# An outer-product recurrence and a bilinear feed-forward in one kernel: weights put together as integers, first units' f loaded whole, and a reordered beginning

## The chip, the cores and the metric

The kernel runs on one core of one Trainium2 chip. A core has a matrix engine (PE, TensorE), a vector engine (DVE), an activation engine (ACT), a general engine (POOL) and a queue engine (SP) that issues most of the transfers. SBUF is the on-chip memory of 128 partitions, PSUM the memory that PE writes to. The metric is device microseconds for one execution, from the first to the last instruction with what lies around it; lower is better.

## The reference

For each of 4 batches and 8 heads a state of 48 by 48 runs through 768 time steps; the outputs of all heads, side by side, are the rows of a feed-forward that multiplies two projections.

```python
f = 1.0 / (1.0 + np.exp(-f_logit))
for t in range(S):
    state = f[:, :, t, :, None] * state + np.einsum('bhd,bhe->bhde', k[:, :, t], v[:, :, t])
    y[:, :, t] = np.einsum('bhd,bhde->bhe', q[:, :, t], state)
x = y.transpose(0, 2, 1, 3).reshape(B * S, H * D)      # 3072 x 384
out = ((x @ w_a) * (x @ w_b)) @ w_out                  # w_a, w_b: 384 x 1536, w_out: 1536 x 384
```

The three weights arrive as 64-bit floats (the random fp32 times a double factor), all else as fp32.

## The kernel before

**The recurrence without a loop over time.** Within a half sequence of 384 steps (BLK), the running product F of f turns the recurrence into plain products: q is multiplied by F, k by a quantity `inv` near 1/F, and then a causal product of q and k (`scores`, masked by `causal`), times v (`within`), plus q times the state at the start of each 64 steps (`across`) gives y. A *unit* is one batch, one half, and four heads (two pairs, the pair on partitions 0 to 47 and 64 to 111). There are 16 units, NQ = 2 of them to a half. Units 0 and 1 are the first halves of batch 0, units 2 and 3 the second halves.

Each unit goes through these steps:

- `front(u)`, a generator in three parts: ACT takes 1 - f and f as two sigmoids (L234, L235) and POOL scales `inv` (L237); DVE scans f into F, in place (L242), and compares its end (`held`, L243); DVE scans `inv` (L252) and multiplies q and k (L253, L254).
- `scores(u)` on PE (L283) and the masking on DVE (L299, tile `at`); `turn(u)`, which transposes k on PE (L310) and copies it with ACT (`kT`, L312).
- `within(u)` on PE (L363); `gains(u)`: PE computes what each 64 steps add to the state (L329), and DVE sums these one after the other into `st` (L343, L345), scaled at the end of a first half by F's last value (L352).
- `across(u)` on PE (L384); ACT copies y out of PSUM (four or three copies, L396), and transfers carry y into `xT`, the transposed input of the feed-forward (L410). For units 0 and 1 some of these are issued by ACT, all others by SP.

**The feed-forward.** A block is one half of one batch: 384 rows. `up(blk, ft)` makes the two projections for 128 of the 1536 columns: 3 + 3 matmuls in fp32, which PE runs as 12 instructions (L426), into two PSUM banks out of four that `scores`, `turn` and `within` of the first units share. `product()` copies one with ACT (`b_sb`, L441) and multiplies on DVE (L446). `down` multiplies pairs of 128 rows by w_out in Strassen-like combinations (L483, L478).

**The weights.** [...]each weight is taken from its two 32-bit words. A list `todo` of 20 pieces, (w_b, w_a) by turns and then w_out, is loaded by `load_weights` into `raw` buffers (L166). `from_double` is a generator of two parts. The first: ACT takes the magnitude of the high word scaled down (L179), its sign (L180), and from that the sign bit (L182); POOL cuts it off at a maximum (L185). The second, on DVE: shift by three and or in the sign (L188), take the exponent (L192), multiply the low word by it (L194), and add (L195). `begin(n)` runs the first part of pieces up to n, `end(n)` the second, and `end` also orders the next load.

**The order.** `tc.manual_schedule()` means that each engine runs its instructions in the order in which the program names them. The beginning, L565 to L651, is written out by hand. After it the list `rest` names all further `up` and `down` calls; its first entry is up(1, 0). Between them, `beside()` takes attention steps out of a queue by due time, and `end(6 + ...)`, `product()` and `begin(...)` keep the weights going, about one piece for each `up`. [...]SP holds an issue back until one of eight transfer semaphores is free, so that eight transfers of SP's and ACT's queues are under way at most.

Of the kernel before, what the change touches and what calls it, by code (L numbers as in the profile page):

```python
# [24 lines left out]
R = 64  # L25
# [53 lines left out]
def by_quotients(ctx, tc, q, k, f_logit, v, moe_w_a, moe_w_b, moe_w_out, out, ident, weights, bad):  # L79
# [8 lines left out]
    NTG = BLK // 128  # L88
    NU = B * NH * NQ
    NBLK = B * NH  # L90
    NSET = 3

# [23 lines left out]
    less = fixed([128, 1], "less")  # L116
    sign = fixedp.tile([128, PIECE], BF16, tag="sign", name="sign")
# [8 lines left out]
    def load_unit(u, names="fkqv"):  # L126
# [4 lines left out]
        cols = slice(half * BLK, half * BLK + BLK)  # L131
        for nm, src in (("f", f_logit), ("k", k), ("q", q)):
            if nm not in names:
                continue
            heads = src[b].rearrange("(n two) d s -> two d n s", two=2)
            for par in range(2):
                nc.sync.dma_start(out=t[nm][R * par:R * par + D], in_=heads[par][:, 2 * qd:2 * qd + 2, cols])
# [15 lines left out]

    todo, raws, going = list(pieces()), [], []
    ended = [0]

    def load_weights(n=1):
        for _ in range(n):
            if len(raws) == len(todo):
                return  # L160
            dst, src, (k, m) = todo[len(raws)]
            raw = dst
            if src.dtype != FP32:
                raw = raw_pool.tile([128, PIECE], mybir.dt.uint64, tag="raw", name="raw")[:, 0:k * m]
                raw = raw.rearrange("p (k m) -> p k m", k=k)
            nc.sync.dma_start(out=raw, in_=src)  # L166
            raws.append(raw)

    def from_double(dst, raw, k, bit):

# [8 lines left out]
        nc.scalar.activation(h, hi.bitcast(FP32), AF.Abs, scale=HI_SCALE)  # L179
        nc.scalar.activation(sgn, hi.bitcast(FP32), AF.Sign)  # L180
# [4 lines left out]
        nc.gpsimd.tensor_scalar(h, h, HI_MAX, None, ALU.min)  # L185
        yield
        hu = h.bitcast(U32)
        nc.vector.scalar_tensor_tensor(  # L188
            out=hu, in0=hu, scalar=3, in1=bit, op0=ALU.logical_shift_left, op1=ALU.bitwise_or
        )  # L190

        nc.vector.tensor_scalar(bit, hu, 0xFF800000, None, ALU.bitwise_and)  # L192
        h, lo, power = (x.rearrange("p (k n) -> p k n", k=k) for x in (h, lo, bit.bitcast(FP32)))
        nc.vector.scalar_tensor_tensor(out=dst, in0=lo, scalar=2.0**-52, in1=power, op0=ALU.mult, op1=ALU.mult)  # L194
        nc.vector.tensor_tensor(dst, h, dst, ALU.add)  # L195
        yield

    def begin(n):

        while len(going) < min(n, len(todo)):  # L200
            i = len(going)
            dst, src, shape = todo[i]
            going.append(from_double(dst, raws[i], shape[0], bits[i % len(bits)]) if src.dtype != FP32 else iter(()))
            next(going[i], None)

    def end(n):

        while ended[0] < min(n, len(todo)):
# [3 lines left out]
            if ended[0] > 2:  # L212
# [10 lines left out]
    live = {}  # L223
    xT = {}
# [4 lines left out]
    def front(u):  # L229

        t = sets[u % NSET]
        x = halves(t["f"])
        inv = sb2.tile([128, 2 * BLK], FP32, tag="inv", name="inv")
        nc.scalar.activation(inv, x, AF.Sigmoid, bias=less, scale=-1.0, accum_out=tails[:, u:u + 1])  # L234
        nc.scalar.activation(x, x, AF.Sigmoid)  # L235
# [4 lines left out]
        for n in range(2):  # L240
            c = slice(n * BLK, n * BLK + BLK)
            nc.vector.tensor_tensor_scan(x[:, c], x[:, c], none, math.exp(MIDDLE), ALU.mult, ALU.add)  # L242
        nc.vector.tensor_tensor(held[:, u], t["f"][:, :, BLK - 1], least, ALU.is_ge)  # L243
# [3 lines left out]
        nc.vector.reciprocal(start, t["f"].rearrange("p n (c m) -> p n c m", m=C)[:, :, 0:NC - 1, C - 1])  # L247
# [5 lines left out]
        nc.vector.tensor_tensor(halves(t["q"]), halves(t["q"]), x, ALU.mult)  # L253
# [63 lines left out]
    def gains(u):  # L317
# [3 lines left out]
        last = half == NH - 1  # L321
        for n in range(2):
            for c in range(NC):
                for p in range(2):
                    if last and c == NC - 1 and p == 1:
                        continue
                    for h in range(2):
                        r = slice(SUB * p, SUB * p + SUB)
                        nc.tensor.matmul(  # L329
                            ps_x[R * h:R * h + D, p, (n * NC + c) * D:(n * NC + c) * D + D],  # L330
                            lhsT=kT[r, n, c, R * h:R * h + D],
                            rhs=t["v"][r, n, c, h * D:h * D + D],
                            start=True,
                            stop=True,
                        )
        st = sb3.tile([128, NJ, 2, D], FP32, tag="st", name="st")
        before = live[u - NQ]["st"][NJ] if half else None
        live[u]["st"] = [before]
        for j in range(NJ - 1 if last else NJ):
            c, p = divmod(j, 2)  # L340
            new = ps_x[:, p, 0:2 * NC * D].rearrange("r (n c d) -> r n c d", n=2, c=NC)[:, :, c]
            if before is None:
                nc.vector.tensor_copy(st[:, j], new)  # L343
            else:
                nc.vector.tensor_tensor(st[:, j], before, new, ALU.add)  # L345
            before = st[:, j]
            live[u]["st"].append(before)
        if not last:

            for n in range(2):  # L350
                end = t["f"][:, n, BLK - 1:BLK]
# [20 lines left out]
    def across(u):  # L372
# [22 lines left out]
        for p, e, r, rows in (*whole, (1, R, 0, D), (1, 0, R, D)):  # L395
            nc.scalar.copy(y[r:r + rows, :, p], ps[p][e:e + rows, 0:BLK].rearrange("r (o m) -> r o m", m=SUB))  # L396
# [19 lines left out]
    HFT = NFT // 2  # L416
# [109 lines left out]
    def slot(u):  # L526
# [19 lines left out]
        next(nxt, None)  # L546
        yield
# [17 lines left out]
    with tc.manual_schedule():  # L565
        nc.scalar.preload_act_table_set("sigmoid_and_others")
        for x, value in ((less, -K_EXP), (zero, 0.0), (least, math.exp(MIDDLE - DECAY_MAX)), (ones, 1.0)):
            nc.gpsimd.memset(x, value)
        for n, x in (("f", 30.0), ("k", 0.0), ("q", 0.0)):
            for u in range(NSET):  # L570
                eng = nc.vector if n == "f" or n == "q" and u == 0 else nc.gpsimd
                eng.memset(sets[u][n], x)
        for ps in (ps_x, ps_y):
            nc.scalar.copy(ps[:, :, 0:BLK], zero.unsqueeze(1).broadcast_to((128, 2, BLK)))
        load_unit(0, "f")
        load_unit(1, "f")
        load_unit(0, "kqv")
        load_unit(1, "kqv")
        load_weights(2)
        load_unit(2)  # L580
        load_weights(2)


        fronts = [front(u) for u in range(2 * NQ + 1)]
        next(fronts[0])
        next(fronts[1])
        for bit in bits:
            nc.gpsimd.memset(bit, 0)
        make_identity(nc, ident)
        nc.gpsimd.memset(causal, 1.0)  # L590
        for p in range(2):
# [3 lines left out]
            )  # L595
        next(fronts[0])
        next(fronts[0])
        next(fronts[1])
        scores(0)
        turn(0, True)  # L600
        begin(2)
        next(fronts[1])
        within(0)
        gains(0)
        next(fronts[2])
        scores(1, True)
        turn(1, True)
        across(0)
        within(1, True)
        end(1)  # L610
        gains(1)
        across(1)
        for u in range(NQ):
            load_unit(u + NSET)
            load_weights()
        end(2)
        begin(3)


        next(fronts[2])  # L620
        next(fronts[2])
        scores(2)
        turn(2, True)
        next(fronts[3])
        begin(4)
        within(2)
        end(3)
        gains(2)
        up(0, 0)
        across(2)  # L630
        next(fronts[3])
        product()
        end(4)
        begin(5)
        up(0, 1)
        next(fronts[3])
        product()
# [439 lines left out]
```

## Time and profile before

| | us |
|---|---|
| median of three runs (653.26 to 655.56) | 655.42 |
| the profiled execution, its own time | 657.89 |
| its span | 656.1 |
| PE busy | 618.1 (94%) |
| weight loads of PE busy | 446.9 (68%) |
| DVE busy | 327.7 (50%) |
| ACT busy | 174.9 (27%) |
| POOL busy | 68.9 (10%) |

The profile records one execution. A row of its instruction groups gives line, engine, operation and tiles, then how many, their busy time, the mean of one in ns, and the engine's idle time just before them with what ended it. A line of the chain of work gives a start, a length and what ran. The busy times by stretch give, after the stretch and its length, PE, weight loads, DVE, ACT and POOL, each with its count of instructions, then the granted clock of PE, the share of the transfer engines and their GB/s. Matmul records overlap, so a group's mean is longer than the distance from one matmul to the next. Idle time of an engine that nobody waits for costs nothing.

### The profile page before, as it was taken

The numbers are of one execution on the slowest core, as the hardware profiler recorded it, in microseconds if no ns is written. First come the engines' busy times: TensorE is split into PE (matmuls) and PEld (weight loads), VectorE is DVE, ScalarE is ACT, GpSimd is POOL, SyncE is SP. The second block draws the span as 40 slices with busy tenths as digits, with TensorE's granted clock in tenths as the row PEclk, the third lists the DMA queues.
The fourth block names the chain that finished last, engine by engine and source line by source line (L and its number), as shares of the span: only waits on it lengthen the run. The fifth ranks groups of instructions, "written<-read, shape, count | busy, mean of one in ns | idle before, by whom it ended". The sixth has DMA issues, their size and how long they took to land.

```text
span 656.1 us, 12293 instructions
## 1 busy us (share of the span) xinstructions
PE 618.1 (94%) x5202; PEld 446.9 (68%) x5202; DVE 327.7 (50%) x610; ACT 174.9 (27%) x312; POOL 68.9 (10%) x57
## 2 busy tenths in 40 slices
PE   1667899999999999999999999999999999999996
PEld 1554555557898666966699666865689655865696
DVE  7878699995875345351443244443363121311241
ACT  3564677531321222122200312122200122011100
POOL 6232365410110000000000000000000000000000
PEclk9966999999999999999999999999999999999999
DMA  8688556100144124040210033140000000000000
GB/s 209 172 207 238 164 169 221 68 0 1 37 106 116 37 55 91 15 104 1 63 32 35 25 79 71 22 115 0 20 1 24 26 19 19 0 26 0 1 24 30
DMA packets 30209, 43.37 MB, mean 66 GB/s; under 512 B 3776, under 2 KB 24768, under 8 KB 30144
## 3 DMA queue, kind: packets, MB, share of 16 engines
q1 hardware_dynamic: 29856, 42.19, 23.7%
q8 instruction: 43, 0.70, 0.5%
q10 hardware_dynamic: 288, 0.30, 0.2%
q14 instruction: 22, 0.18, 0.1%
HBM read 33.03 MB, written 4.72 MB: 58 GB/s over the span
## 4 chain that ended last, share of the span: by engine, by line
PE 90%; DVE 5%; DMA 2%; ACT 1%; issue 1%; POOL 0%; ACTq 0%; SPq 0%; DVEq 0%
PE f L426 57%; PE f L483 24%; PE ps_x L283 2%; PE ps_y L363 2%; PE ps_y L384 2%; PE ps_x L329 1%; DMA xT<-y 1%; DVE inv L252 1%; PE ps_x L310 1%; DVE f_in L242 1%; PE f L310 1%; DVE k_in L254 1%; DMA f_in<-in_f_logit_dram 0%; DVE h L478 0%; DVE q_in L253 0%
## 5 line engine op out<-in xcount | busy, mean ns | idle before, releaser
L426 PE MATMUL f<-xT,w_a 128*128 128x384 f32 x576 | 203.6, 490 | 5.6 <-DVE start L247 4.6
L426 PE MATMUL f<-xT,w_b 128*128 128x384 f32 x576 | 205.7, 494 | 0.0
L426 PEld LDWEIGHTS f<-xT,w_a 128*128 128x128 f32 x576 | 110.1, 191 | 83.2 <-issue 6.4
L426 PEld LDWEIGHTS f<-xT,w_b 128*128 128x128 f32 x576 | 107.8, 191 | 70.4 <-issue 1.2
L446 DVE TENSOR_TENSOR ab<-f,b_sb 128x384 f32<-128x384 f32 x96 | 53.0, 554 | 180.4 <-PE f L426 130.1
L441 ACT COPY b_sb<-f 128x384 f32<-128x384 f32 x96 | 46.0, 479 | 238.9 <-PE f L426 225.8
L483 PE MATMUL f<-raw,h 128*128 128x192 f32 x432 | 73.7, 328 | 0.0
L483 PEld LDWEIGHTS f<-raw,h 128*128 128x128 f32 x432 | 70.2, 190 | 0.5
L483 PE MATMUL f<-w_out,ab 128*128 128x192 f32 x288 | 51.1, 327 | 0.9 <-DVE u L478 0.9
L237 POOL TENSOR_SCALAR inv<-inv 128x768 f32<-128x768 f32 x16 | 16.3, 1020 | 328.1 <-ACT inv L234 328.1
L185 POOL TENSOR_SCALAR h<-h 128x768 f32<-128x768 f32 (+1 forms) x20 | 44.0, 2202 | 61.3 <-ACT h L179 61.3
L483 PEld LDWEIGHTS f<-w_out,ab 128*128 128x128 f32 x288 | 47.4, 190 | 3.0 <-DVE u L478 1.2
L478 DVE TENSOR_TENSOR o<-f,u 128x192 f32<-128x192 f32 x36 | 12.9, 357 | 56.6 <-PE f L483 56.4
L283 PE MATMUL ps_x<-q_in,k_in 48*64 48x64 f32 x720 | 16.2, 238 | 22.1 <-DVE k_in L254 22.1
L283 PEld LDWEIGHTS ps_x<-q_in,k_in 48*64 48x64 f32 x720 | 14.6, 151 | 23.9 <-POOL causal L590 13.9
L242 DVE TENSOR_TENSOR_SCAN f_in<-f_in,zero 128x384 f32<-128x384 f32 x32 | 28.8, 941 | 3.1 <-POOL inv L237 3.1
L299 DVE TENSOR_TENSOR at<-ps_x,causal 128x768 f32<-128x768 f32 x15 | 14.4, 958 | 31.4 <-PE ps_x L283 31.3
L252 DVE TENSOR_TENSOR_SCAN inv<-inv,start,zero 128x128 f32<-128x128 f32 x64 | 27.5, 470 | 0.0
L345 DVE TENSOR_TENSOR st<-st,ps_x 128x96 f32<-128x96 f32 x80 | 20.3, 253 | 12.1 <-PE ps_x L329 9.6
L483 PE MATMUL f<-raw,ab 128*128 128x192 f32 x144 | 25.7, 328 | 0.0
L483 PE MATMUL f<-w_out,h 128*128 128x192 f32 x144 | 25.4, 326 | 0.0
L396 ACT COPY y<-ps_y 48x384 f32<-48x384 f32 (+1 forms) x45 | 21.4, 475 | 11.1 <-PE ps_y L384 10.0
(82 smaller groups left out, 477.1 us busy)
## 6 DMA issues: line engine op xcount, KB each, us to landing
f_in<-in_f_logit_dram SPq DMA_DIRECT2D x32, 144.0 KB, 3.2
k_in<-in_k_dram SPq DMA_DIRECT2D x32, 144.0 KB, 3.6
q_in<-in_q_dram SPq DMA_DIRECT2D x32, 144.0 KB, 3.9
v_in<-in_v_dram SPq DMA_DIRECT2D x16, 288.0 KB, 4.2
raw<-in_moe_w_out_dram SPq DMA_DIRECT2D x6, 768.0 KB, 4.3
out_dram<-o SPq DMA_DIRECT2D x24, 192.0 KB, 1.9
raw<-in_moe_w_b_dram SPq DMA_DIRECT2D x5, 768.0 KB, 7.4
raw<-in_moe_w_a_dram SPq DMA_DIRECT2D x5, 768.0 KB, 6.2
```

The source lines that it names most:

```text
L185: nc.gpsimd.tensor_scalar(h, h, HI_MAX, None, ALU.min)
L237: nc.gpsimd.tensor_scalar(inv, inv, EXP_K, 1.0, ALU.mult, ALU.add)
L242: nc.vector.tensor_tensor_scan(x[:, c], x[:, c], none, math.exp(MIDDLE), ALU.mult, ALU.add)
L252: nc.vector.tensor_tensor_scan(inv[:, w], inv[:, w], none[:, 0:C], first, ALU.mult, ALU.add)
L283: nc.tensor.matmul(ps[h][SUB * p:SUB * p + SUB, o:o + SUB], lhsT=kf[r, tokens(n, c, p)], rhs=qf[r, tokens(n, c, p)], start=True, stop=True,)
L299: nc.vector.tensor_tensor(to, x, tri.broadcast_to((128, *lead, 2 * NC, SUB)), ALU.mult)
L345: nc.vector.tensor_tensor(st[:, j], before, new, ALU.add)
L396: nc.scalar.copy(y[r:r + rows, :, p], ps[p][e:e + rows, 0:BLK].rearrange("r (o m) -> r o m", m=SUB))
L426: nc.tensor.matmul(ps[nm], lhsT=w[:, kt, ft * 128:ft * 128 + 128], rhs=x[:, kt], start=kt == 0, stop=kt == NKT - 1,)
L441: nc.scalar.copy(b_sb, ps["b"])
L446: nc.vector.tensor_tensor(products[blk, part][:, :, i], a, b, ALU.mult)
L483: nc.tensor.matmul(to, lhsT=x[:, i], rhs=w[:, i], start=first and i == 0, stop=i == HFT - 1, skip_group_check=True)
```

## The change

- **Weights as integers.** The low word is turned into a small integer by one more activation on ACT (Identity, with scale 2^-29 and bias 2^23, so that the rounded value sits in the low bits of the result); the sign bit is then written into the upper half of the same word. DVE shifts the high word by three and adds the two as 32-bit integers. DVE has two instructions for a piece where it had four. The compiled program has the integer add as one instruction over 16-bit halves. `from_double` has three parts now, and `begin` counts half pieces.
- **f of units 0 and 1 loaded whole.** Their f is read with 64 rows for each head instead of 48 (the 16 more are the next head's), so the tile needs no memset before. F of these units goes to a tile of its own, `firsts`, out of the ab pool, and ACT makes it before `inv`. POOL sets the f tiles to 30 before units 3 and 4 are loaded.
- **States summed in PSUM.** For units 0 to 3 `gains` accumulates on PE the whole sum from the start of the half for each 64 steps (6 matmul pairs where there were 3). For units 0 and 1 ACT copies the sums in two instructions; for units 2 and 3 DVE adds the state before in two instructions.
- **Two early pieces.** Pieces 4 and 5 are loaded into buffers of the ab pool instead of raw buffers.
- **The y copies** of the second part of units 0 and 1 are made by DVE instead of ACT.
- **The beginning.** Loads, fronts, weights and units are put into another order; `front` has one more part (q and k by themselves).

```diff
     def from_double(dst, raw, k, bit):
...
         nc.scalar.activation(h, hi.bitcast(FP32), AF.Abs, scale=HI_SCALE)
+        nc.scalar.activation(bit.bitcast(FP32), lo, AF.Identity, bias=whole, scale=2.0**-29)
+        nc.gpsimd.tensor_scalar(h, h, HI_MAX, None, ALU.min)
+        yield
         nc.scalar.activation(sgn, hi.bitcast(FP32), AF.Sign)
         nc.scalar.activation(
             bit.bitcast(U16).rearrange("p (n two) -> p n two", two=2)[:, :, 1], sgn, AF.Relu, scale=-32768.0
         )
-        nc.gpsimd.tensor_scalar(h, h, HI_MAX, None, ALU.min)
         yield
         hu = h.bitcast(U32)
-        nc.vector.scalar_tensor_tensor(
-            out=hu, in0=hu, scalar=3, in1=bit, op0=ALU.logical_shift_left, op1=ALU.bitwise_or
-        )
-        nc.vector.tensor_scalar(bit, hu, 0xFF800000, None, ALU.bitwise_and)
-        h, lo, power = (x.rearrange("p (k n) -> p k n", k=k) for x in (h, lo, bit.bitcast(FP32)))
-        nc.vector.scalar_tensor_tensor(out=dst, in0=lo, scalar=2.0**-52, in1=power, op0=ALU.mult, op1=ALU.mult)
-        nc.vector.tensor_tensor(dst, h, dst, ALU.add)
+        nc.vector.tensor_scalar(hu, hu, 3, None, ALU.logical_shift_left)
+        hu, bit = (x.rearrange("p (k n) -> p k n", k=k) for x in (hu, bit))
+        nc.vector.tensor_tensor(dst.bitcast(U32), hu, bit, ALU.add)
         yield
```

```diff
+        if u - NSET in FIRST and "f" in names:
+            nc.gpsimd.memset(t["f"], 30.0)
...
+            if nm == "f" and u in FIRST:
+                for par in range(2):
+                    row = ((b * H + 4 * qd + par) * D) * S + half * BLK
+                    rows = bass.AP(src.tensor, src.offset + row, [[S, R], [2 * D * S, 2], [1, BLK]])
+                    nc.sync.dma_start(out=t[nm][R * par:R * par + R], in_=rows)
+                continue
...
     def front(u):
+        if u in FIRST:
+            nc.scalar.activation(F, x, AF.Sigmoid)
         nc.scalar.activation(inv, x, AF.Sigmoid, bias=less, scale=-1.0, accum_out=tails[:, u:u + 1])
-        nc.scalar.activation(x, x, AF.Sigmoid)
+        if u not in FIRST:
+            nc.scalar.activation(x, x, AF.Sigmoid)
...
     def gains(u):
+        whole_sums = u < 2 * NQ
...
+                        parts = [(c, slice(SUB * p, SUB * p + SUB))]
+                        if whole_sums:
+                            parts = [(i, slice(0, C)) for i in range(c)] + [(c, slice(0, SUB * p + SUB))]
...
+        if whole_sums:
+            for p in range(2):
...
+                if before is None:
+                    nc.scalar.copy(to, new)
+                else:
+                    nc.vector.tensor_tensor(to, new, before.unsqueeze(2).broadcast_to((128, 2, nc_p, D)), ALU.add)
...
     def across(u):
-            nc.scalar.copy(y[r:r + rows, :, p], ps[p][e:e + rows, 0:BLK].rearrange("r (o m) -> r o m", m=SUB))
+            copy = nc.vector.tensor_copy if u in FIRST and p else nc.scalar.copy
+            copy(y[r:r + rows, :, p], ps[p][e:e + rows, 0:BLK].rearrange("r (o m) -> r o m", m=SUB))
```

The beginning as it is after the change (before, it is L574 to L651 of the listing above):

```python
        load_unit(0, "f"); load_unit(0, "q"); load_weights(); load_unit(1, "f")
        next(fronts[0]); load_weights(); load_unit(0, "k")
        next(fronts[0]); load_weights()
        next(fronts[0]); load_unit(1, "k"); patterns(); load_unit(1, "q"); load_unit(0, "v")
        next(fronts[1]); load_unit(2, "k"); load_unit(2, "f"); load_unit(2, "v")
        next(fronts[0]); scores(0); begin(3); turn(0, True); load_unit(1, "v"); load_weights()
        next(fronts[1]); within(0); next(fronts[1]); gains(0)
        next(fronts[2]); next(fronts[1]); load_weights(); across(0)
        next(fronts[2]); load_weights(); turn(1, True); scores(1, True); end(2); within(1, True)
        load_unit(2, "q"); load_unit(NSET, "f"); gains(1); across(1); end(3)
        next(fronts[2]); next(fronts[2]); begin(4.5)
        up(0, 0); load_weights(); product(); end(4)
        next(fronts[3]); turn(2, True); scores(2, True); next(fronts[3])
        up(0, 1); end(5)
        load_unit(NSET + 1, "v"); load_unit(NSET + 1, "k"); load_unit(NSET, "v"); load_weights()
        load_unit(NSET, "q"); load_unit(NSET, "k"); end(6); product(); begin(7); load_unit(NSET + 1, "q")
        within(2); gains(2); load_unit(NSET + 1, "f"); next(fronts[3]); next(fronts[3])
        up(0, 2); product(); across(2); up(0, 3); scores(3); begin(8); turn(3, True); end(7)
        within(3); gains(3); across(3); end(8); product(); up(0, 4); product()
```

## The prediction

> **What bounds the kernel now.** I read the page's slices first, then the chain that ended last, then the busy time by stretch, then the instructions in order of time up to 100 us.
>
> ```profile
> PE   1667899999999999999999999999999999999996
> DVE  7878699995875345351443244443363121311241
> ACT  3564677531321222122200312122200122011100
> PEclk9966999999999999999999999999999999999999
> ```
>
> One slice is 16.4 us. TensorE (PE) is full from the fifth slice to the end; before that it is not, and its granted clock dips in slices three and four. The chain and the stretches:
>
> ```profile
> 27.95 3.87 DMA xT<-y
> 43.34 4.51 PE f L426 x12
> 50.95 4.60 DMA xT<-y
> 74.67 79.57 PE f L426 x246
> ```
>
> ```profile
> 30.00:43.00 13.00, 5.19 (x140) 4.75 (x142) 11.01 (x21) 7.14 (x12) 3.31 (x2) 0.52 0.61 147
> 80.00:155.00 75.00, 75.00 (x279) 44.21 (x277) 68.30 (x88) 42.30 (x60) 29.03 (x14) 1.00 0.34 107
> ```
>
> From 74.67 us the chain is one run of matmuls. In 80 to 155 us (columns: PE, weight load, DVE, ACT, POOL) PE is busy 75.00 of 75.00 us, while DVE, busy 68.30 of 75, does not hold it. So easing DVE after 80 us buys nothing; only the time at which PE becomes continuous counts. My milestone is the start of up(1,0), the first of the list `rest`: 80.55 us before. All behind it, to 656.1, is 575.55 us, the same PE work in both kernels. Before 80 us the chain runs through DVE, y, and the xT transfers.
>
> The durations I use:
>
> ```profile
> L179 ACT ACTIVATE h<-raw 128x768 f32<-128x768 f32 x7 | 6.3, 902 | 2.1 <-issue 1.9 <-DMA raw<-in_moe_w_a_dram 0.2
> L188 DVE SCALAR_TENSOR_TENSOR h<-h,bit 128x768 uint32<-128x768 uint32 x5 | 4.7, 949 | 0.0
> L192 DVE TENSOR_SCALAR bit<-h 128x768 uint32<-128x768 uint32 x5 | 3.3, 661 | 0.2
> L195 DVE TENSOR_TENSOR w_a<-h,w_a 128x768 f32<-128x768 f32 x2 | 1.9, 957 | 0.1
> 45.75 2.10 PE L426 MATMUL f<-xT,w_a 128*128 128x384 f32 x6
> 55.41 4.18 PE L426 MATMUL f<-xT,w_a 128*128 128x384 f32 x6 [4.60 <-DVE start L247]
> ```
>
> The last two are the same six matmuls: warm they follow each other at 0.32 us, after an idle gap at 0.64.
>
> **What the skill says.** "TensorE: Matmul & The Clock Gate", Part 1: the clock is halved after an idle window of about 3.4 us and returns after about as long busy. The trace agrees on the factor; after the gap at 50.8 to 55.4 it took about 9 us to return. "ScalarE: Activation LUTs", What ACT_TABLE_LOAD costs: every function runs at 0.833 ns an element, about 0.28 us on top with a pointer bias; Identity at 768 is so estimated at 0.92 us, and the Abs row shows 0.90. "VectorE: DVE Perf Modes", The perf-mode tier table: fp32 tensor_scalar runs at twice tensor_tensor's rate; the rows show 0.56 (undisturbed) against 0.96.
>
> **A weight piece (768 columns).** DVE before: 0.95+0.56+0.96+0.96 = 3.43 us. After: the shift, priced as L192's 0.56 us, and the integer add. The add works on 16-bit halves, 1536 of them; two at a time it costs L195's 0.96, one at a time 1536 at about 1 ns, some 1.8. I take 0.96, as the same page's table gives two-source 16-bit work two a cycle; so 1.5 us, at worst 2.4. ACT gains an Identity. Its steps were 0.82, 0.97 and 1.07 us; one more of 0.82 makes 3.68 (384 columns: 1.59 to 2.05). POOL's min is unchanged. For 80 to 155 us, ACT per up-step is 3.68+0.48 (b_sb) = 4.16 us against PE's 12 matmuls in 3.87. It falls 0.3 us behind in each of four steps, regains 2.5 in the two half-size pieces, then loses 0.3 in each of six: at most 2 us late. A factor's two PSUM banks are wanted again only two ups later, so b_sb may be some 5 us late: hidden, and PE stalls beyond that.
>
> **The beginning, step by step.** SP need no longer wait for the f memsets, so f0 is issued at 0.75, not 1.74. Rows are 64 instead of 48: 393 KB for a unit instead of 295. Once the rings are full, SP's issues, each held until an earlier transfer lands, follow at about 0.70 us for 147 KB; I use 0.93 for a whole f half, 1.25 for a 393 KB weight piece, 2.4 for 786 KB, 0.95 for v, and 2.0 us before the first. f0 lands at 4.6 (before 5.1). F0 is now ACT's first activation, so the scan starts at 5.5 instead of 7.2. But k0 is now behind q0, w_b0, f1 and w_a0 and lands at 11.8: k's product ends at 12.9, scores(0) starts at 13.0 (before 13.9). Gain 0.9.
>
> Now the waits that are added. v0 is queued behind w_b1 (786 KB), k1 and q1: it lands at 18.0 (before by 10.5), so within(0) starts at 18.0 (before 17.0). ACT has three pieces ahead of kT0: inv1 ends at 11.0, then 2.05+2.05+3.6 ends at 18.65, w_b1 landing at 14.2; kT0 ends at 19.6 (before 17.6). Whole sums double gains(0): 48 to 96 PE instructions, 1.19 to 2.4 us at the low clock, 19.5 to 21.9. ACT's two state copies (0.4 each, between the 0.32 and 0.48 rows) end at 22.8; they replace six DVE steps of 1.66. On DVE the scaling of st waits for them, with q1 and k1 behind it: k1 ends at 25.1 (before 21.1). Scores(1) ends at 28.4, at1 at 29.5, within(1) at 31.0, gains(1) at 33.4, st1 34.3, across(1) 35.75 (before 29.85). Two y copies go to DVE, beside ACT's two: 36.9 instead of 34.1. ACT's xT issues wait for DVE's y copies, with kT1 behind them in unit 0 (29 us, covered by at1). SP stands at xT too from 18.5 to 26.2; w_a2, q2 and f3 behind it land by 34, wanted from 40. xT of unit 1 is issued from 36.95 to 38.85 and lands at about 40.9.
>
> So the start of up(0,0) moves from 43.3 to 41, but scores, turn, within and gains of unit 2 (5.4 us on PE) now stand behind it. PE has idled from 35.75 and starts cold: some eight matmuls at 0.64 and four at 0.32, it ends at 47.4. From there PE has turn(2) 0.8, scores 0.85, up(0,1) 3.9, within 0.85, gains 1.05, up(0,2) 3.9, across 0.9, up(0,3) 3.9, scores(3) 0.8, turn 0.8, within 0.85, gains 1.05, across 0.9, together 20.55 us. DVE in between: product 0.55, w_a1 1.5, at 1.0, f3 1.9, w_b2 1.5, w_a2 (ACT ready at 54.7) to 55.8, product, two state sums 0.75, unit 3's front 4.0, ending at 61.15, before PE wants it at 63.6. PE waits 0.2 for w_a1 and about 1.1 around at3, w_b3 and st3. Across(3) ends at 69.25 (before 71.5). The state sums as two wide adds save 0.65 of 1.41 us twice; gains(2) and (3) grow by 32 instructions, 0.5 us each.
>
> Last: xT of unit 3. From across to its landing took 6.7 us in unit 2 (48.7 to 55.4), by y copies and five issues of 0.57 on SP. Before, up(0,3) and up(0,4) covered it; now up(0,4) alone (69.25 to 73.1). So up(1,0) starts at 69.25+6.7 = 76.0, PE idle 2.9 us, under a whole idle window. Sum: 80.55 - 76.0 = 4.55 us gained. The span becomes 651.6; the profiled execution took 657.89, 1.8 around its span and 2.5 over the median, so the median 655.42 becomes 650.9.
>
> At nothing: the POOL memsets before f3 and f4 (0.7 us each; POOL is at three tenths and the loads lead by 10 us); the two early pieces in ab buffers (a buffer's next user comes after 50 us); the split q/k step of front (same instructions in the same order).
>
> **Rivals.**
> B, more: PE warms inside one window of up(0,0) and unit 3's transfer lands in 5.5 us. 2.4+1.2 us earlier: 647. For it: xT landed 1.8 us after issue at best. Against: the 9 us warm-up.
> C, the gain is eaten: PE stays at half clock through up(0,0) to up(0,1), as it did from 55.4 to 65. Up(0,0) 7.7 and up(0,1) 7.7 instead of 6.4 and 3.9, less the waits this covers: 3.5 us, 654.4.
> D, slower: the DMA queue becomes the bound. 3.83 MB now stand up to v0, and after 38 us 4.6 MB up to k3, wanted at 60. I took 250 GB/s; the trace has 251 in 10 to 20 us and 287 in 43 to 55, but 209 over the first 16.4. At 190 GB/s v0 comes 4 us later, k3 at 64 instead of 56, and up(1,0) at 84: 659. It is slower from about 190 down.
> That ACT becomes the bound after 80 us needs Identity at 1.4 us or more; at twice the adopted price the early gain is gone as well. The nearest row is against it.
>
> **How the numbers follow.** Mine 0.52 (648.5 to 653.5), B 0.22, C 0.12, D 0.14. A measurement here tells about 0.5%, 3.3 us, from no change: B and three quarters of mine are faster (0.61), the rest of mine and C the same (0.25), D slower (0.14). The add at 1.8 us instead of 0.96 puts st3 and across(3) about 1 us later, inside mine. 646 to 657 leaves out D and little else.
>
> **What would show it.** scores(0) near 13.0; kT0 near 19; across(1) ending near 36, later than before; up(0,0) near 41 with matmuls at 0.64; up(1,0) near 76, released by xT; in 80 to 155 us DVE near half busy, ACT near full, PE without a gap. Wrong if v0 lands well after 20 us, if the add's row shows 1.8 us, if PE shows gaps released by b_sb after 80 us, or if up(0,1) is still at 0.64.

## The result

The changed kernel takes 673.99 us (median of four runs, 672.72 to 676.98), the kernel before 655.49 beside it (653.26 to 656.49): a ratio of 1.0294, 95% interval 1.0251 to 1.0336. It is slower by 18.5 us where 4.5 us of gain were forecast. Its profiled execution has a span of 672.1 us.

The page's slices of the changed kernel, one slice being 16.8 us:

```profile
PE   1797999999999999999999999999999999999995
DVE  4436534448777443624173243624173121311241
ACT  6316739873222132221310132221310021101100
PEclk9999999999999999999999999999999999999998
```

PE looks better in the beginning than before (its third slice is 9 where it was 6), and DVE, at 7 and 8 in the first four slices before, is down to 3 to 6. Nothing here says "slower". Nor can the row PEclk be taken as it stands: the trace has its first clock record at 63.3 us (in before at 27.1), and the page prints full clock for the time ahead of it. The same 48 matmuls of `scores` show the pace (start, length, what; unit 1, then unit 2):

```profile
34.43 1.56 PE L308 MATMUL f<-q_in,k_in 48*64 48x64 f32 x48
63.80 0.93 PE L308 MATMUL f<-q_in,k_in 48*64 48x64 f32 x48
```

In what follows "cold" is the slow pace, ahead of the first record or where a record says 0.50, and "warm" the full one.

The chain of work that ended last says what became slower:

```profile
20.44 8.95 PE ps_x L358 x96
...
38.63 8.95 PE ps_x L358 x94
...
69.62 4.53 PE ps_x L358 x72
...
85.97 4.55 PE ps_x L358 x71
...
95.75 2.23 DMA xT<-y
98.03 72.61 PE f L465 x224
```

L358 is the matmul of `gains`. In before its stretches were too short to matter on the chain. PE's timeline of before has these for units 0 and 3:

```profile
18.30 1.19 PE L329 MATMUL ps_x<-v_in,kT 64*48 64x48 f32 x48
68.44 0.70 PE L329 MATMUL ps_x<-v_in,kT 64*48 64x48 f32 x40
```

And that of the changed kernel for units 0 and 2:

```profile
20.19 9.19 PE L358 MATMUL ps_x<-v_in,kT 64*48 64x48 f32 x96
69.44 4.71 PE L358 MATMUL ps_x<-v_in,kT 64*48 64x48 f32 x72
```

On the chain the four have 8.95, 8.95, 4.53 and 4.55 us, 27.0 in all. PE is busy in the early slices because it runs these.

The waits of the changed kernel (who waits for what: us in total, times, the longest) show what is behind them:

```profile
ACT st L374 <- PE ps_x L358: 19.8, 2, 10.4
DVE st L391 <- ACT st L374: 18.2, 2, 9.6
```

ACT stands with the copy of the sums until PE is through, and DVE stands behind ACT, with the products of q and k of the next unit queued after it. Up(1,0), the milestone of the prediction, starts at 96.1 us instead of the 76.0 forecast (80.55 before). Behind it lie 576.0 us (672.1 - 96.1), before it was 575.55.

The busy times by stretch (PE, weight load, DVE, ACT, POOL with their counts, then clock, transfer share, GB/s):

```profile
80.00:155.00 75.00, 73.40 (x425) 44.57 (x424) 32.88 (x50) 54.36 (x79) 26.86 (x14) 1.00 0.45 134
100.00:155.00 55.00, 55.00 (x172) 32.22 (x171) 27.23 (x41) 45.87 (x65) 24.73 (x13) 1.00 0.40 126
```

From 100 to 155 us PE is busy 55.00 of 55.00 us while ACT has 45.87 and DVE 27.23: ACT did not become the bound. What the change costs lies ahead of up(1,0), all but about half a microsecond in these two traces.

The groups of instructions of the changed kernel that the prediction priced:

```profile
L199 ACT ACTIVATE bit<-raw,whole 128x768 f32<-128x768 uint32 x14 | 14.0, 1001 | 0.0
L209 DVE TENSOR_SCALAR h<-h 128x768 uint32<-128x768 uint32 x16 | 9.3, 583 | 0.0
L211 DVE CUSTOM_DVE_ANT_0 w_b<-h,bit 128x1536 uint16<-128x1536 uint16 x5 | 4.8, 959 | 0.5 <-DVE h L209 0.2
L358 PE MATMUL ps_x<-v_in,kT 64*48 64x48 f32 x624 | 22.3, 216 | 0.0
L358 PE MATMUL ps_x<-v_in,kT 128*48 128x48 f32 x240 | 19.6, 259 | 0.0
```

And the row of before from which the price of `gains` came:

```profile
L329 PE MATMUL ps_x<-v_in,kT 64*48 64x48 f32 x704 | 13.3, 220 | 0.0
```

Identity 1.00 us (0.92 estimated, and 0.82 in the sum for a piece), the shift 0.58 (0.56), the integer add 0.96 (0.96). The last two of the five rows are the surprise: 240 instructions with weights of 128 rows are new, and even the 64-row ones, of which there are fewer than before (624 against 704), keep PE busy for 22.3 us where all 704 took 13.3.

### The profile page after: what moved, and what is told of

The parts are those of the page before. It is cut to its first block, busy times and chain, and to the rows that moved or that the text cites. A ratio compares the mean times of both kernels' runs of the same rounds, so it can differ in the third digit from the quotient of the medians.

```text
span 672.1 us, 12560 instructions
## 1 busy us (share of the span) xinstructions
PE 640.0 (95%) x5362; PEld 462.8 (69%) x5362; DVE 285.4 (42%) x554; ACT 188.0 (28%) x332; POOL 65.2 (10%) x58
## 4 chain that ended last, share of the span: by engine, by line
PE 93%; DMA 3%; DVE 1%; SPq 1%; issue 0%; ACT 0%; ACTq 0%; DVEq 0%
PE f L465 56%; PE f L522 25%; PE ps_x L358 5%; PE ps_y L402 2%; PE ps_y L423 2%; PE ps_x L308 1%; PE ps_x L335 1%; DMA xT<-y 1%; DMA v_in<-in_v_dram 1%; DMA raw<-in_moe_w_a_dram 1%; SPq L145 0%; DVE y L436 0%; PE f L402 0%; DVE f_in L266 0%; PE f L423 0%
## 5 line engine op out<-in xcount | busy, mean ns | idle before, releaser
L261 POOL TENSOR_SCALAR inv<-inv 128x768 f32<-128x768 f32 x16 | 17.9, 1118 | 332.7 <-ACT inv L257 332.7
L200 POOL TENSOR_SCALAR h<-h 128x768 f32<-128x768 f32 (+1 forms) x20 | 40.4, 2018 | 75.5 <-ACT h L197 75.4
L358 PEld LDWEIGHTS ps_x<-v_in,kT 64*48 64x48 f32 (+1 forms) x864 | 30.0, 135 | 10.8 <-issue 5.6
L358 PE MATMUL ps_x<-v_in,kT 64*48 64x48 f32 (+1 forms) x864 | 37.0, 228 | 0.0
L308 PE MATMUL ps_x<-q_in,k_in 48*64 48x64 f32 x672 | 13.6, 226 | 14.3 <-DMA raw<-in_moe_w_b_dram 14.3
L266 DVE TENSOR_TENSOR_SCAN f_in<-f_in,zero 128x384 f32<-128x384 f32 x28 | 25.2, 941 | 0.0
```

The source lines that it names most:

```text
L261: nc.gpsimd.tensor_scalar(inv, inv, EXP_K, 1.0, ALU.mult, ALU.add)
L266: nc.vector.tensor_tensor_scan(F[:, c], F[:, c], none, math.exp(MIDDLE), ALU.mult, ALU.add)
L308: nc.tensor.matmul(ps[h][SUB * p:SUB * p + SUB, o:o + SUB], lhsT=kf[r, tokens(n, c, p)], rhs=qf[r, tokens(n, c, p)], start=True, stop=True,)
L358: nc.tensor.matmul(ps_x[R * h:R * h + D, p, (n * NC + c) * D:(n * NC + c) * D + D], lhsT=kT[r, n, ci, R * h:R * h + D], rhs=t["v"][r, n, c ...
```

## The experiments

In each run the kernel before ran beside it on the same chip; ratios are to those runs. A chain of reasons was at stake: is it the `gains` matmuls or the new order (the first run); if the matmuls, is it their accumulation, the 128 rows of their weights, or something else (the runs on accumulation, rows, heads and height); and what are the other parts of the change worth (the rest).

### Without the whole sums

```diff
-        whole_sums = u < 2 * NQ
+        whole_sums = False
```

> The changed kernel with the states of units 0 to 3 summed on VectorE again, as units 4 on do; all else as changed. Theory M, the miss is the gains matmuls themselves: gains(0), (1) go from 9.19 and 8.95 us back to about 1.2, gains(2), (3) from 4.53 and 4.55 to 0.7, and six VectorE steps of 0.25 us replace two state steps of 0.70 to 0.72 in all, so 8.0 + 7.7 + 2 x 3.8 - 4 x 0.8 = 20 us less: 654, between 650 and 657. Rival R, the reordered beginning and late loads are what costs: gains shrink but PE then waits for v, the weight pieces or xT, and the time stays above 665.

651.83 us, ratio 0.9923 (0.9893 to 0.9952). Its timeline has the `gains` of unit 0:

```profile
19.58 1.21 PE L358 MATMUL ps_x<-v_in,kT 64*48 64x48 f32 x48 [0.45 <-ACT kT L337]
```

and its chain the end of the beginning:

```profile
36.89 4.75 DMA xT<-y
41.78 4.44 PE f L465 x8
...
69.67 3.75 DMA xT<-y
73.55 73.22 PE f L465 x226
```

PE's timeline has the start of up(1,0) ahead of its wait for xT:

```profile
71.89 0.81 PE L465 MATMUL f<-xT,w_b 128*128 128x384 f32 x2
```

One line of the change undone takes away the whole loss, and the time comes near the forecast (650.9, which is 0.9931 of before), though that was made for the kernel with the sums. Up(0,0) runs its first matmuls at 34.31 and has all of xT at 41.78 (41 forecast); up(1,0) starts at 71.89 and goes on at 73.55 (76.0 forecast). Rival R, that order and loads are what costs, is out: they are all still there.

### Accumulation, rows, and the order of the heads

Three edits of `gains` in the changed kernel:

```diff
 # no accumulation
-                                start=i == 0,
-                                stop=i == len(parts) - 1,
+                                start=True,
+                                stop=True,
```

> The changed kernel with every matmul of gains starting its address anew: the same 96 instructions with the same 128-row and 64-row operands in the same order, but nothing accumulates (the states are wrong: the sum over the chunks is left out). T1, the weights that fill all 128 rows are the cause: still 90 to 95 ns an instruction, gains(0) about 9 us, and about 674 in all. T2, accumulating to one address serialises: about 25 ns each, gains(0) 2.4 us, and about 655 in all.

```diff
 # 64 rows alone
-                            parts = [(i, slice(0, C)) for i in range(c)] + [(c, slice(0, SUB * p + SUB))]
-                        for i, (ci, r) in enumerate(parts):
+                            parts = range(2 * c + p + 1)
+                        for j in parts:
+                            q = j % 2
+                            r = slice(SUB * q, SUB * q + SUB)
...
-                                ps_x[R * h:R * h + D, p, (n * NC + c) * D:(n * NC + c) * D + D],
+                                ps_x[R * h:R * h + D, q, (n * NC + c) * D:(n * NC + c) * D + D],
...
```

> The changed kernel with each whole sum of units 0 to 3 made of 64-row matmuls alone, upper and lower rows alternating into two banks (the two banks are not added together, so the states are wrong): 168 instructions for a first half instead of 96, still accumulating to one address within a bank. T1: 168 at 25 ns cold, gains(0) about 4.2 us, and 168 at 17.5 ns warm less the last chunk's, gains(2) about 2.7; in all about 660. T2: 45 to 93 ns each, gains(0) 8 to 15 us, and 673 or more in all.

```diff
 # heads alternate
-                    for h in range(2):
-                        parts = ...
-                        for i, (ci, r) in enumerate(parts):
+                    parts = ...
+                    for i, (ci, r) in enumerate(parts):
+                        for h in range(2):
```

> The changed kernel with the loop over the two heads moved inside the loop over the parts, so that consecutive matmuls alternate between the two halves of the columns; sums and operands are the same. T1 in its strict form (weights on all rows never overlap the running matmul): still about 93 ns, gains(0) 9 us, 674. T1 in its weaker form (only weights on the same rows and the same columns exclude each other): about 45 ns or less, gains(0) 4.5 us, about 662. T2: two addresses alternate, about 47 ns, the same as the weaker form; the run without accumulation tells these two apart.

The `gains` of unit 0 in the timeline of the run without accumulation:

```profile
20.51 9.19 PE L358 MATMUL ps_x<-v_in,kT 64*48 64x48 f32 x96
```

In that of the run with 64 rows alone, weight loads first:

```profile
21.12 3.04 PEld L360 LDWEIGHTS ps_x<-v_in,kT 64*48 64x48 f32 x120
21.22 3.06 PE L360 MATMUL ps_x<-v_in,kT 64*48 64x48 f32 x119
26.95 1.07 PE L360 MATMUL ps_x<-v_in,kT 64*48 64x48 f32 x49 [2.66 <-issue]
```

And in that of the run with alternating heads:

```profile
19.50 5.95 PE L358 MATMUL ps_x<-v_in,kT 64*48 64x48 f32 x96
```

Without accumulation the stretch is 9.19 us to the last digit, and the time 672.65: T2 is out. With 64 rows alone, 119 instructions take 3.06 us, 26 ns each, and they do accumulate: so more instructions, and accumulation, at the old price. That run took 668.15 us, not the 660 expected: it has 168 instructions for a first half, and in three of its four stretches PE stopped once for 1.8 to 2.7 us with nothing that the profile shows to wait for ("issue"). The traces have a hint: in each of the three, PE goes on 1.4 to 1.6 us after a transfer of 16 KB on queue 8, which the page calls "instruction", has landed (landed at 25.56, 64.29 and 79.53, PE on at 26.95, 65.67 and 81.16). The other stops of this kind over 0.6 us, five in all the traces here, end 1.3 to 1.6 us after such a landing as well. That PE had run out of instructions fits this; no run tests it.

Alternating heads gave 5.95 us, 62 ns each, and 661.59 us: between the two forms of T1. So T1 was not the whole of it. The start times of the single matmuls in the traces say more. Worked out from these, the step from one start to the next, by the rows of the two matmuls (count x mean ns):

```
                              64 to 64   64 to 128   128 to 64   128 to 128
before, gains(0)              47 x 19    -           -           -
changed, gains(0)             14 x 84    10 x 208    9 x 210     62 x 61
changed, gains(2), warm       15 x 52     8 x 135    8 x 138     40 x 38
heads alternate, gains(0)     18 x 40     6 x 208    5 x 210     66 x 40
```

In before, groups of four (by the order of the program two heads with two instructions each, on one half of the rows) start 6 or 7 ns apart, and the next four, on the other half, 60 ns later. In the changed kernel every change between 64 and 128 rows takes 208 or 210 ns cold, and the step or two just after a change are slow as well (about 115 ns). Another 18 of the 62 steps from 128 to 128 rows take 80 ns; why is not shown. Alternating the heads also happened to take away 8 of 19 changes. This made a new theory, S: the change of height is a cost of its own.

### Sorted by height

The whole sums are put into a list, and the list is sorted so that a unit's 64-row matmuls all come first; in the second run the heads alternate within it as well.

```diff
+        jobs = []
...
+                            jobs.append((n, c, p, h, i, ci, r, i == len(parts) - 1))
+        if whole_sums:
+            jobs.sort(key=lambda x: x[6].stop - x[6].start)
...
```

> The changed kernel with the matmuls of its whole sums sorted by their height: in each unit all those of 64 rows first, then all those of 128; sums and operands are the same. From the start times in the changed kernel's trace a step between matmuls of different height took 208 to 210 ns cold (19 of them in gains(0), 4.0 us of 8.9) and 135 to 138 warm (16 in gains(2), 2.2 us of 4.5); one from 128 rows to 128 rows 61 and 38 ns. Theory S, changing the height is a cost of its own: gains(0) 24 x 40 + 72 x 61 + 210 ns = 5.6 us, gains(2) 24 x 26 + 48 x 38 + 140 ns = 2.6 us, 10.6 us less in all: about 663. Theory W, the width of 128 rows is the whole cost and the steps only fall at those places: gains(0) stays near 9 us and the time near 674.

```diff
-            jobs.sort(key=lambda x: x[6].stop - x[6].start)
+            jobs.sort(key=lambda x: (x[6].stop - x[6].start, x[0], x[1], x[2], x[4], x[3]))
```

> The same, and the two heads alternate among the matmuls of 128 rows as in the run with swapped heads, where a step from 128 rows to 128 took 40 ns cold and 24 warm. Theory S: gains(0) 24 x 40 + 72 x 40 + 210 ns = 4.0 us, gains(2) 24 x 26 + 48 x 24 + 140 ns = 1.9 us, 15 us less than the changed kernel: about 659, still slower than the run without whole sums. Theory W: the 5.95 us that alternating heads alone gave, or more; about 662.

Unlike what the first expectation says, the sums of these two runs are not those of the changed kernel: the output is 6% off. Several sums of one bank are open at the same time there; the Trainium skill, "PSUM — Partial Sum Buffer", The four PSUM rules, states that a second group's first matmul then makes the first group's next one overwrite instead of adding, and lost parts of the sums would fit that. So the two runs price an order of instructions, and are no usable kernel. The instructions and their shapes are those of the changed kernel.

The `gains` of units 0 and 2 in the timeline of the first run:

```profile
20.15 4.43 PE L363 MATMUL ps_x<-v_in,kT 64*48 64x48 f32 x96
...
58.73 1.95 PE L363 MATMUL ps_x<-v_in,kT 64*48 64x48 f32 x72
```

And those of unit 0 in the timeline of the second:

```profile
20.10 3.67 PE L363 MATMUL ps_x<-v_in,kT 64*48 64x48 f32 x96
```

The same 96 instructions, with one change of height instead of 19, take 4.43 us instead of 9.19; the time falls to 658.27 us (one run), with alternating heads to 656.27 beside 656.08 of before. Theory S holds, and by more than it expected: the steps from 128 to 128 rows fall from 61 to 43 ns too, since the slow ones after a change and most of those of 80 ns are gone. W, the width alone, is out. What is left is a lower rate at one height: cold steps of 40 ns among the 64-row matmuls, which here use one half of the rows alone (19 where both halves take turns), and of 43 among those of 128 rows.

The 3.67 us of the second run owe more to the clock than to the heads: its first clock record is at 22.9 us, inside this stretch, and its steps from 128 to 128 rows are 40 ns before that and 22 after. In unit 1, cold in both runs almost to its end, they are 43 ns without and 39 with alternating heads.

Even at its best the whole sum costs PE 3.67 us where the single sums cost 1.2, and by the ratios the kernel without sums is still 3 to 5 us faster.

### The sums alone, in the order of before

The kernel before, with the changed `gains`.

> The kernel before with the whole sums of units 0 to 3 alone. Theory M: the same four stretches of gains grow to 9, 9, 4.5 and 4.5 us also in this order, some 23 us more on PE less about 3 us of state steps; PE's idle time in the beginning lies elsewhere in the chain, so 14 to 20 us slower than before's run beside it. If the new order had made them slow, gains stay near 2.4 us each and the time within 3 us of before's.

676.80 us (one run) beside 655.11: 21.7 us slower, a little above the range expected. Its chain:

```profile
18.72 8.94 PE ps_x L333 x96
...
51.96 7.09 PE ps_x L333 x72
...
84.36 4.54 PE ps_x L333 x72
```

The same stretches, in another order; the one at 51.96 has a granted clock of 0.50 on record and takes 98 ns an instruction where the one at 84.36, at 1.00, takes 63. The price belongs to the instructions, not to their place.

### What the integer weights are worth

First the kernel without whole sums, with the four VectorE operations of before (L188 to L195 of the listing) in place of the two; then the kernel before with the integer weights alone.

```diff
-        nc.scalar.activation(bit.bitcast(FP32), lo, AF.Identity, bias=whole, scale=2.0**-29)
...
-        nc.vector.tensor_scalar(hu, hu, 3, None, ALU.logical_shift_left)
-        nc.vector.tensor_tensor(dst.bitcast(U32), hu, bit, ALU.add)
+        (the four operations of before)
```

> The run without whole sums, with the weights put together by the four VectorE operations of the kernel before (and no Identity on ScalarE). VectorE gets 3.43 us for a full piece instead of 1.5, eight pieces up to the start of up(1,0), 13.5 us more in a stretch where it had about 15 us idle. Theory V, the integer weights are what lets the new beginning run: the three pieces ahead of the sums of unit 2 and the two ahead of those of unit 3 push across(2) and across(3), and up(1,0) starts 6 to 9 us later than the 73.5 of the run without sums; about 659. Rival O, the order and the whole f make the gain and VectorE's idle time covers the four operations: within 2 us of the run without sums.

> The kernel before with the integer weights alone, in its own order (the Identity is issued with the other ScalarE steps of a piece). Up to 80 us VectorE is relieved of 5 x 1.93 + 2 x 0.97 = 11.6 us and ScalarE gets 6 us more. Theory V: part of that lies on the chain of the beginning, so up(1,0) starts 3 to 6 us earlier than 80.5 and the time is 3 to 6 us under before's; after 80 us the relief of VectorE buys nothing. Rival O: the beginning of before waits for loads and for the order of its steps, and the time is within 2 us of before's.

The first: 660.51 us, ratio 1.0066 (1.0043 to 1.0088), by the ratios 7.5 to 9.4 us above the kernel without sums; the new beginning with the old weights is slower than before. PE's timeline has the place:

```profile
65.03 1.81 PE L427 MATMUL ps_y<-q_in,st 48*48 48x64 f32 x48 [4.12 <-DVE st L388]
...
79.00 1.16 PE L427 MATMUL ps_y<-q_in,st 48*48 48x64 f32 x48 [3.02 <-DVE st L388]
```

PE stands 4.12 and 3.02 us at `across` of units 2 and 3 for the sums of states, which are behind two and one weight pieces of 3.4 us on DVE: the two places that theory V named.

The second: 650.86 us, ratio 0.9914 (0.9885 to 0.9943). Up(1,0) starts at 74.03 in its timeline, 6.5 us earlier than in the trace of before, which is of an execution 2.4 us over its median:

```profile
74.03 2.10 PE L423 MATMUL f<-xT,w_b 128*128 128x384 f32 x6
```

So the integer weights, which the prediction took for a support of the new order, give the gain by themselves. To see what the order adds, both ran again side by side:

> The kernel without whole sums once more, beside the other two on one chip, to tell what the new order and the whole f add to the integer weights. Theory V, nearly all of the gain is the integer weights': within 2 us of the kernel before with the integer weights alone. Rival O: the order adds 3 us or more of its own.

> The kernel before with the integer weights alone once more, beside the kernel without whole sums: 650 to 652 where before's runs have 655; theory V has the other within 2 us of it, rival O has it 3 us or more above.

The kernel without sums: 0.9952 (0.9935 to 0.9970) in 19 runs; before with integer weights alone: 0.9945 (0.9927 to 0.9962) in 15. Beside the integer weights, the new order, the whole f, the y copies and the early pieces together add nothing that can be measured.

### Loads behind xT

In the run without sums xT of unit 1 takes 4.75 us of the chain above, and PE idles for 2.55 of them. Two small transfers on SP that read xT keep SP from issuing more loads before it has landed:

```diff
         across(1)
+        landed = fixed([128, NKT], "landed")
+        for kt in range(NKT // 2, NKT):
+            nc.sync.dma_start(out=landed[:, kt:kt + 1], in_=xT[0][:, kt, 0:1])
         end(3)
```

> The run without whole sums, with two transfers of 512 bytes on SP's queue that read xT of unit 1, so that SP issues no further loads until that xT has landed. Without them xT of unit 1 lands 4.75 us after its last issue, while three weight loads of 786 KB are issued from 36.3 to 38.3 us. Theory Q, these loads hold the xT transfer: it lands 2.2 to 2.8 us after its last issue and up(0,0) starts near 39.4 instead of 41.8; the time falls by up to 2.4 us, less what the later loads cost. Rival: the landing stays at 4.5 us or more and the time is the same or longer.

649.31 us, ratio 0.9891 (0.9863 to 0.9919), which overlaps with the interval of the run without the gate (0.9893 to 0.9952). PE's timeline without the gate, then with it:

```profile
41.78 1.62 PE L465 MATMUL f<-xT,w_b 128*128 128x384 f32 x2 [2.55 <-DMA xT<-y]
```

```profile
40.75 3.18 PE L465 MATMUL f<-xT,w_b 128*128 128x384 f32 x4 [1.66 <-DMA xT<-y]
```

Without the gate PE waited twice for xT in up(0,0), the second time for the last of five transfers, of 72 KB: it landed 4.75 us after its issue began (4.78 in the other run of the same kernel). With the gate it landed in 2.14 us, and the second wait is gone: the last two of these matmuls start 3.6 us after DVE's second y copy has ended (42.31 against 38.74), without the gate 6.2 (41.78 against 35.61). Its profiled execution, at 652.54 us the longest of its five, shows where some of this goes again:

```profile
70.98 5.69 DMA xT<-y
...
76.81 13.33 PE f L465 x40
```

That is xT of unit 3, behind loads that were pushed back. A second gate, the loads of units 5 and 6 behind it, and ScalarE's queue for some of the five transfers should take that away:

```diff
-                    queue = nc.scalar if u < NQ and (n + h) % 2 else nc.sync
+                    queue = nc.scalar if u < 2 * NQ and (n + h) % 2 else nc.sync
...
         across(3)
+        for kt in range(NKT):
+            nc.sync.dma_start(out=landed[:, kt:kt + 1], in_=xT[1][:, kt, 0:1])
         end(8)
+        load_unit(2 + NSET)
+        load_unit(3 + NSET)
```

> The run with the gate behind xT of unit 1, and the same for unit 3: the loads for units 5 and 6 and one weight piece, which were issued ahead of and right behind that unit's xT, wait until it has landed, and ScalarE's queue issues two of the five xT transfers of units 2 and 3. In the profiled execution of the first gate xT of unit 3 landed 5.69 us after its last wait, behind loads that the gate had pushed back, and PE waited 2.80 us for it. Theory Q: with that wait gone (0.85 us left, as without gates, or less) and up(0,0) at 2.0 us behind the last y copy, the time is 646 to 649.5 and below both other runs of this call by 1.5 us or more. Rival: what the gates hold back is wanted soon after, and the time is that of the run without gates, within 1 us.

649.75 us, ratio 0.9908 (0.9880 to 0.9937), 3 us under the two runs beside it and just outside the range named. PE's timeline has up(0,0) and the steps around unit 3:

```profile
38.93 3.17 PE L465 MATMUL f<-xT,w_b 128*128 128x384 f32 x4 [1.66 <-DMA xT<-y]
...
64.93 0.85 PE L358 MATMUL ps_x<-v_in,kT 64*48 64x48 f32 x40 [0.71 <-ACT kT L337]
67.00 1.81 PE L423 MATMUL ps_y<-q_in,st 48*48 48x64 f32 x48 [1.22 <-DVE st L384]
68.73 4.21 PE L465 MATMUL f<-xT,w_b 128*128 128x384 f32 x6
```

The last transfer of unit 1's xT lands in 2.14 us again, and the wait for xT of unit 3 is gone. But ScalarE, now with three issues of 0.6 us ahead of a weight piece (the expectation has two), brings `kT` of unit 3 late (0.71 us), and after these short waits up(0,4) runs its first six matmuls in 4.21 us instead of 2.20, with a granted clock of 0.50 on record from 66.2 to 73.1 us. No gain of the second gate over the first can be measured. The kernel with one gate and no whole sums has the lowest ratio here, 0.9891; it is not clear of two gates (0.9908), nor of the integer weights alone beside it (0.9914).

## Why the prediction was wrong

**The step that failed** is "Whole sums double gains(0): 48 to 96 PE instructions, 1.19 to 2.4 us at the low clock", and with it "gains(2) and (3) grow by 32 instructions, 0.5 us each" (the 1.05 us in the sum of PE). It took the price of an instruction, 25 ns, from a row with 64-row weights and gave it to a mixture of 64 and 128 rows. The four stretches were put at 2.4 + 2.4 + 1.05 + 1.05 = 6.9 us and have 27.0 on the chain. That is 20.1 us, and up(1,0) came 96.1 - 76.0 = 20.1 us later than forecast (that the two agree so closely is chance: other steps were off as well). With the sums undone up(1,0) starts 24.2 us earlier, at 71.9. Of the 6.8 us too little for unit 0, the changes of height, with the slow steps that go with them, are 4.8 (9.19 against 4.43 when sorted), and the lower rate at one height is the other 2.0.

The row was not of the same kind: its form, `64*48`, stands in the profile, and the diff has slices of a whole chunk, 128 rows, in the new `parts`. Nor were the new costs bounded from both sides there, as was done for the integer add. The Trainium skill has both halves of it, and the operation was not taken for a new one: "TensorEngine Tiling (Array Packing)", Key Properties, says "Mode switching requires drain", which agrees with the 208 ns cold and 135 ns warm here, figures that it does not give; "TensorE: Matmul & The Clock Gate", Part 3, The mechanism, says that a weight load overlaps a running matmul only where the row groups differ, which agrees with the mean steps of 19 ns where both halves of the rows take turns, against 40 ns where only one is used and 39 to 43 where every matmul takes all rows.

**The place of the cost** follows the prediction's own chain: it had the state copies of ACT behind `gains`, the scaling on DVE behind them and q1 and k1 behind that. These waits came as described, and long: 9.4 and 10.4 us of ACT, 8.6 and 9.6 of DVE.

**Right, as the traces show.** The scan of F started at 6.2 us (5.5 forecast). V0 was wanted at 18.0 and came at 18.8. Behind up(1,0) the trace has 576.0 us where before had 575.55. The shift and the integer add came at the prices taken. PE ran cold into up(0,0), and was warm one `up` later.

**Wrong without weight.** Scores(0) was to gain 0.9 us and lost 0.4 (14.30 against 13.91), since k0 landed at 12.8 instead of 11.8. Rival D foretold a slower kernel, by transfers: the rate up to 16.4 us was 225 GB/s and v0 was 0.8 us late, not four; it had the sign and not the cause. Rival C's half clock through up(0,1) did not come. The prediction also quotes that the full clock returns after about 3.4 us of busy PE; in the changed kernel PE is busy by its records from 20.2 to 29.4 us without a gap, and the first full clock on record comes at 63.3 us.

**Near in number, in part by luck.** Without the sums the kernel has 0.9923 and, measured again, 0.9952 of before, where 0.9931 was forecast for the kernel with them; its up(1,0), past the wait for xT, is at 73.55 us in one trace and at 76.93 in the other (76.0 forecast). The gain was worked out for order and weights together and never split. The runs show that it is the integer weights', which give the same gain in the order of before (0.9945 against 0.9952), and that the order without them is slower (1.0066). That "easing DVE after 80 us buys nothing" was right (behind up(1,0) the kernel before with integer weights alone has 575.9 us, before 575.55), and what it eases ahead of 80 us is the gain.

## What to carry to other kernels

The price of one instruction may be taken from a row only if the new instructions have that row's shape, and if their neighbours do: on PE what stands before a matmul can cost more than the matmul. When small matmuls are merged into taller ones, sort them by height, but mind which sums of one PSUM bank are open at the same time, and count what the two halves of the rows did by turns before. A clock of 1.00 ahead of the first clock record says nothing: compare the durations of like matmuls. And when a change has several parts, work out each alone; here one part carried the gain, one lost several times as much, and the rest added nothing to it.

## What the runs showed of the hardware

- A change between matmuls of 64 and of 128 rows cost 208 to 210 ns from start to start cold and 135 to 138 warm, in both directions, with the next step or two slow as well. In runs of matmuls of one height the mean steps were 19 to 43 ns cold.
- Accumulating to one PSUM address, matmul after matmul, cost nothing in the order of the changed kernel: 9.19 us with and without it.
- Small 64-row matmuls ran at 19 ns from start to start cold where the two halves of the rows take turns, and at 40 ns where only one half is used; those of 128 rows at 39 to 43 ns, with the column halves taking turns or not. Warm these were 13, 22, and 23 to 24 ns.
- In the changed kernel PE is busy by its records through the 9.2 us of gains(0), and the first full clock on record comes at 63.3 us. With the same matmuls sorted by height it came at 24.4 and 22.9 us, within gains(0). Why is not shown.
- With 168 small matmuls in a row, PE stopped once for 1.8 to 2.7 us in three of four stretches with no wait on record, each time until 1.4 to 1.6 us after an instruction transfer of 16 KB had landed.
- An xT transfer of 72 KB landed 4.75 and 4.78 us after its issue began beside three loads of 768 KB, and in 2.14 us in both runs that held these back.
